# Late attention rows in four banks, the first weight prepared earlier, float32 rows for two second groups

## The chip, the cores and the metric

The kernel runs on one core of a Trainium2 chip. Its engines are TensorE (PE in the profile; its weight loads are PEld), VectorE (DVE), ScalarE (ACT), GpSimd (POOL) and SyncE (SP), which issues most of the transfers. The metric is the device time of one execution in microseconds. The kernel before took 896.62 us as the median of three runs (895.96 to 898.36).

## What is computed

Three stages follow each other. N is 2304 tokens, in 18 tiles of 128.

```
a    = softmax(phi over the 576 positions)           # 4 batches, 8 heads, 32 memory slots
k_m, v_m = a^T k, a^T v
x    = softmax(q k_m^T / 8) v_m                      # 2304 x 512
noisy = x w_gate + log1p(exp(x w_noise)) * noise     # 2304 x 8
top 2 of 8 experts for each token, weights by softmax over the two
y    = sum over the two: weight * relu(x w1[e]) w2[e]    # w1 512 x 1024, w2 1024 x 512
h    = y w_in;  out = (h * cos h) w_out              # w_in 512 x 2048, w_out 2048 x 512
```

Wide products run as three float16 products: each operand is split into a high and a low half, and high*high, high*low and low*high are added.

## The kernel before

**Attention.** `k_gen(b)` builds the memory of a batch; `t_gen(t)` takes a tile of tokens through eight steps: scores on TensorE (`sc`, L734), maximum and subtraction on VectorE (L739, L742), exponential on ScalarE, row sums and reciprocal on VectorE (L747, L748), division on GpSimd (`d`, L750), transposes on TensorE (`pt`), and the product with the values (`x`, L764), whose last 16 columns of each half are the logits of the gate. `x` lies in one tile of two PSUM banks. ScalarE then copies the row (`xs`, L769) and the logits (`lgb`, L775), writes the high half (`hl`, L780), GpSimd subtracts for the low half (L782), and SyncE stores both halves as one row of 2 KB in the DRAM tensor `xd` (L783).

**Routing.** `route(g)` works for two groups of tokens, tiles 0 to 7 (group 0) and 8 to 17 (group 1). On VectorE it is a chain of some thirty small instructions on 64 or 80 elements per partition (L420 to L482), broken by an exponential and a logarithm on ScalarE and by three rank products on TensorE (L461 to L463), which wait for `m16` (L453). Then one-hot matrices (`oha`, L496; `ohp`, L501, two for each tile) are multiplied on TensorE (`tab`, L505) into lists of token numbers: `idxA` (L510) at the end of group 0, `idxB` (L513) at the end of group 1. The first 256 tokens of each expert come from group 0 (part 0), the next 352 from both groups (part 1).

**First expert.** `gather_x(0, 0)` fetches the rows that `idxA` names (GpSimd issues one indirect DMA for 128 rows, L913), and SyncE issues DMA transposes into `xT` (L916). `l1(0, 0, f)` for f = 0 to 7 issues 12 products `h` each (four k, three half-products). Their weight is `wt[0]`: squares of `raw` on ScalarE (`w_square`, into `junk`), a sum on TensorE (`sums`), four tiny instructions for the scale (`norm_scale`), four high quarters on ScalarE (`w_hi`) and four low quarters on VectorE (`w_lo`, x4). `l1_out` applies relu on ScalarE and takes the low half on VectorE (`hT`). `l2_first` multiplies by the second weight `wt[1]`, whose `w_lo` run at 120.31 us. Then come `gather_x(0, 1)` and `l1(0, 1, f)`, the same for part 1, and seven more experts, whose weights are prepared beside the products.

**What sets the order.** Closures are put on a list with a time (`at`), and issued in the order of that time; `lead` raises an instruction's priority. `gated(key)` makes what is issued inside it come after the instruction noted in `last[key]`; `chain(key, ...)` keeps a whole sequence in order on its engine. So each engine has one fixed order of instructions, and an instruction whose operand is late holds everything behind it on its engine. Around the change the order is set by `t_steps`, `AHEAD`, `e0_after`, the `advance(r0, ...)` lines and the offsets behind `tA`, the nominal end of attention.

**Buffers.** `lp` (`l2k`) has seven slots of 2 KB per partition, which `xs`, `hl`, the junk tile and the outputs share; `wp` has four of 16 KB, for phi, q and the weights. PSUM has eight banks: two `ke`, `kt`, `m`, and until attention ends four for `sc`, `pt` and `x`, which then become `ha`, `hb`, `ya`, `yb`.

Of the kernel before, what the change touches and what calls it, by code (L numbers as in the profile page):

```python
# [39 lines left out]
MAXOV = 28  # L40
Y0 = MAXOV * P
# [24 lines left out]
def fused_kernel(ctx, tc, phiT, qT, kv, wgn, noise, w1, w2, wi, wo, out):  # L66
# [3 lines left out]
    xd = nc.dram_tensor("xd", (N, 2 * DM), F16).ap()  # L70
    yd = nc.dram_tensor("yd", (YROWS, DM), F32).ap()
# [341 lines left out]
    def route(g):  # L413
# [68 lines left out]
        V.scalar_tensor_tensor(pf[:, ts, :], af16[:, ts, :], float(-P), vk, op0=OP.mult, op1=OP.add)  # L482
# [9 lines left out]
        for t in range(t0, t1, 3):  # L492
            m = min(3, t1 - t)
            tt = slice(t, t + m)
            oha = small.tile([P, 3, 2, E * NST], F16, tag="oha", name="oha", bufs=2)[:, :m, :, :nc_]
            V.tensor_tensor(oha, acode[:, None, None, c0:].to_broadcast([P, m, 2, nc_]),  # L496
                            af16[:, tt, :, None].to_broadcast([P, m, 2, nc_]), op=OP.is_equal)
            for q in range(m):
                ohp = small.tile([P, 2, P], F16, tag="ohp", name="ohp", bufs=5)
                for k in range(2):  # L500
                    o = V.tensor_scalar(ohp[:, k], iota_r, pf[:, t + q, k:k + 1], tokb[:, t + q:t + q + 1],  # L501
                                        op0=OP.is_equal, op1=OP.mult)
                    last[f"ohp{g}"] = o
                    with gated(f"t{NT - 1 - (g == 0)}P"):
                        last[f"tab{g}_{t + q - t0}"] = T.matmul(  # L505
                            tb[:, :nc_], lhsT=ohp[:, k], rhs=oha[:, q, k], start=(t + q == t0 and k == 0),
                            stop=(t + q == t1 - 1 and k == 1))
            yield
# [120 lines left out]
    def k_gen(b):  # L629
# [69 lines left out]
        A.activation(bv[:, :, 256:272], pw, AF.Copy)  # L699
# [19 lines left out]

    sds = [ap.tile([P, H, M + 1], F32, name=f"sd{k}", tag=f"sd{k}", bufs=1) for k in range(4)]  # L720
# [7 lines left out]
    def t_gen(t):  # L728

        sc = scb[:, t % 2]  # L730
        for p0, n, b in segs(t):
            c0 = (t % 8) * P + p0
            for c in range(4):
                T.matmul(sc[p0:p0 + n, 64 * c:64 * c + 64], lhsT=qt[t // 8][:, c, c0:c0 + n],  # L734
                         rhs=bdkt[b][:, c, :], start=True, stop=True)
        yield
        sv = sc.rearrange("p (h m) -> p h m", m=M)
        mx = ap.tile([P, H], F32, tag="smx", name="smx")
        V.tensor_reduce(mx, sv, axis=AX.X, op=OP.max)  # L739
        dk = sds[t % 4]  # L740
        dv = dk[:, :, 0:M]
        V.tensor_tensor(dv, sv, mx[:, :, None].to_broadcast([P, H, M]), op=OP.subtract)  # L742
        yield
        A.activation(dv, dv, AF.Exp, scale=0.125)
        yield
        su = ap.tile([P, H], F32, tag="ssm", name="ssm")
# [12 lines left out]
        x = aps.tile([P, 2, 512], F32, tag="x", name="x")  # L759
        with gated(f"t{ahead}T" if ahead else f"tab0_{NA - 1}" if t == NT - 1 else None):  # L760
            for p0, n, b in segs(t):
                pn = slice(p0, p0 + n)
                for g in range(2):
                    last[f"t{t}P"] = T.matmul(x[pn, g, 0:272], lhsT=eT[:, g, pn], rhs=bdv[b][:, g, :], start=True,  # L764
                                              stop=True)
        yield
        xs = l2k([P, DM], F32, "xs")
        with gated(f"t{ahead}E"):
            A.activation(xs.rearrange("p (g d) -> p g d", g=2), x[:, :, 0:256], AF.Copy,  # L769
                                          scale=sT[:, 0, t:t + 1] if len(segs(t)) > 1 else sbs[segs(t)[0][2]][:, 0:1])  # L770
# [4 lines left out]
        last[f"t{t}A"] = A.activation(lgb[g][:, t - GROUPS[g][0]], x[:, :, 256:272], AF.Copy)  # L775
        yield
        hl = l2k([P, 2 * DM], F16, "hl")
        hv = hl.rearrange("p (w d) -> p w d", w=2)
        with gated({NT - 2: f"t{NT - 1}A", NT - 1: "ln"}.get(t)):
            A.activation(hv[:, 0], xs, AF.Copy)  # L780
        with gated("gather" if t >= NT - 2 else None):
            G.tensor_tensor(hv[:, 1], xs, hv[:, 0], op=OP.subtract)  # L782
        SP.dma_start(xd[t * P:(t + 1) * P, :], hl)  # L783
        yield

    def load_small():
# [4 lines left out]
    t_steps = (0.0, 1.1, 2.1, 2.8, 4.6, 7.2, 8.0, 8.4)  # L791
    AHEAD = (9, 10, 11, 13, 14, 15, 16)
# [3 lines left out]
        (w_square, 0): ("t7A", "t8A", "t9A", "t10A"),  # L796
        (w_hi, 0): ("t12A", "t13A", "t14A", "t15A"),
        (w_lo, 0): ("ohp0", "idxA", "idxA", "idxA"),
        (w_square, 1): ("t16A", "ln", "ln", "ln"),
        (w_hi, 1): ("ln", "ln", "ln", "ln"),  # L800
        (w_lo, 1): ("idxB", "idxB", "idxB", "idxB"),
    }

    def e0(fn, i, c):

        with gated(e0_after[fn, i][c]):
            fn(i, c)

    def e0_scale(i):
        with gated(("t11P", "t17P")[i]):  # L810
            sum_up(i, 4)
        norm_scale(i, 4)
# [23 lines left out]
    for i in range(NT):  # L836
        g = t_gen(i)
        stages(g, [a_of(i) + x for x in t_steps[:-1 if i >= NT - 2 else None]])
        if i >= NT - 2:
            at(a_end - 0.4499 + 0.0001 * (i - NT + 2), next, g, None, lead=a_end - 0.45 - a_of(i) - t_steps[-1])  # L840
    R1, tA, LA = a_end - 0.5, a_end - 0.45, 60.0
    r0 = route(0)
    for t, n in ((12, 7), (13, 7), (14, 6)):
        at(a_of(t) + 3.0, advance, r0, n, f"t{t}V", f"bdk{B - 1}V")
    at(a_of(17) + 4.75, advance, r0, 99, "t16V", lead=4.5)
    whole(R1, route, 1)
    for c in range(4):
        at(a_of(7 + c) + 8.0, e0, w_square, 0, c)
        at(a_of(12 + c) + 8.0, e0, w_hi, 0, c)
        at(a_of(17) + 7.3 + 0.01 * c if c < 2 else tA + 0.0001 * c, e0, w_lo, 0, c)  # L850
# [4 lines left out]
        at(tA + (0.0017, 0.0018, 0.0025, 0.0035)[c], e0, w_hi, 1, c)  # L855
        at(tA + 0.0096 + 0.00001 * c, e0, w_lo, 1, c)
    at(a_of(11) + 7.0, e0_scale, 0)
    at(tA + 0.0015, e0_scale, 1)


# [45 lines left out]
    def gather_x(e, part, turn=True):  # L906
# [3 lines left out]
        for c in range(c0, c1):  # L910
            g = xg[e, c] = xp.tile([P, 2 * DM], F16, tag="xg", name="xg", bufs=3)
            col = e * (c1 - c0) + c - c0
            last["gather"] = G.indirect_dma_start(out=g, out_offset=None, in_=xd[0:NA * P] if part == 0 else xd,  # L913
                                 in_offset=bass.IndirectOffsetOnAxis(ap=idx[:, col:col + 1], axis=0))
            if turn:
                tr = SP.dma_start_transpose(out=xT[e, part][:, :, (c - c0) * P:(c - c0 + 1) * P], in_=g)  # L916
        if e == 0:
            last["load"] = tr

# [4 lines left out]
    def l1(e, part, f):  # L924
        n = width[part]
        if f == 0:
# [6 lines left out]
        ph = prod[e, part, f] = bank_h()  # L933
        w = wt[2 * e]
        for k in range(4):
            fs = slice(k * F + f * P, k * F + (f + 1) * P)
            with gated("rank" if f else f"t{NT - 1}P") if (e, part, k) == (0, 0, 0) and f in (0, 1) else nullcontext():
                chain("P", T.matmul, ph[:, :n], lhsT=w[:, 0, fs], rhs=x[:, k, :], start=(k == 0), stop=False)
            chain("P", T.matmul, ph[:, :n], lhsT=w[:, 0, fs], rhs=x[:, 4 + k, :], start=False, stop=False)
            chain("P", T.matmul, ph[:, :n], lhsT=w[:, 1, fs], rhs=x[:, k, :], start=False, stop=(k == 3))  # L940
# [60 lines left out]
    def overflow():  # L1001
# [4 lines left out]
        with tc.For_i(0, n, 1, iteration_sync="staggered") as u:  # L1006
# [4 lines left out]
            for t in range(NT):  # L1011
                for k in range(2):
# [10 lines left out]
            G.indirect_dma_start(out=g, out_offset=None, in_=xd,  # L1023
                                 in_offset=bass.IndirectOffsetOnAxis(ap=io[:, :1], axis=0))
            xh = l2k([P, 8, P], F16, "oxh")
            SP.dma_start_transpose(out=xh, in_=g)
# [236 lines left out]
    at(tA + 0.0094, next_pools)  # L1263
    at(tA, gather_x, 0, 0, lead=LA)
    for f in range(8):
        at(tA + 0.002 + 0.001 * f, l1, 0, 0, f, lead=LA)
        at(tA + 0.002 + 0.001 * f, l1_out, 0, 0, f, lead=LA)
    for c in range(CA):
        at(tA + 0.0095 + 0.003 * c, l2_first, c, False, f"tab1_{NG - 1}", lead=LA)
# [23 lines left out]
    at(x - 0.05, gather_x, 0, 1)  # L1293
    at(x - 0.04, gather_x, 1, 0)
    for e in range(E):
# [15 lines left out]
        if e == 0:  # L1311
            at(x + 0.1, gather_x, 1, 1)
# [134 lines left out]
    OV, LP, PRE = 13.0, 16.0, 30.0  # L1447
    for c in range(2 * NCH):
# [61 lines left out]
```

## Time and profile before

| | us |
|---|---|
| median of three runs | 896.62 (895.96 to 898.36) |
| the profiled execution's own time | 897.48 |
| its span, first to last instruction | 895.5 |
| PE busy in the span | 861.0 (96%) |
| mean granted TensorE clock | 0.978 of full speed |

The span is what the trace shows from the first to the last instruction; the time of the execution is 1.98 us longer. The page shows the span in 40 slices of 22.4 us. Attention ends at 94.3 us, the products of the first expert begin at 103.8 us, and those of its second part at 129.7 us. From 160 us on TensorE has no idle slice before the last one.

### The profile page before, as it was taken

To read this page: it belongs to the slowest core of one execution; us is meant where nothing else is said; L and a number is where in the kernel's file an instruction comes from. 1 tells how busy PE (TensorE), PEld (TensorE's weight loads), DVE (VectorE), ACT (ScalarE), POOL (GpSimd) and SP (SyncE) were. 2 spreads that over 40 slices of the span, in tenths; PEclk is the share of its full clock that TensorE was granted. 3 is DMA by queue.
4 is the path that set the end of the run, shared out by engine and by line. 5 is a ranking of instruction groups with operands and counts; after the bars stand their busy time and mean duration, and the time that the engine had idled before them with its cause. 6 is when DMAs were issued, how large, how long until landed. Compare 5 with 4: busy or idle time off the path is not lost.

```text
span 895.5 us, 16091 instructions
## 1 busy us (share of the span) xinstructions
PE 861.0 (96%) x6328; PEld 523.5 (58%) x6328; DVE 584.1 (65%) x1248; ACT 465.0 (52%) x830; POOL 214.7 (24%) x242
## 2 busy tenths in 40 slices
PE   5997599999999999999999999999999999999997
PEld 3875355757566574757566576654444444444564
DVE  3559853775668576866752389999877654465564
ACT  3588526566677677667762345453434322322233
POOL 1355321110111102010101154443532222222221
PEclk9898599999999999999999999999999999999999
DMA  9982459879989879796963623331522001100001
GB/s 350 395 329 83 129 159 224 293 221 314 221 298 272 275 237 309 251 322 252 258 253 133 196 71 83 71 94 48 119 58 61 25 0 24 48 1 1 1 24 47
DMA packets 109629, 146.66 MB, mean 164 GB/s; under 512 B 65776, under 2 KB 68720, under 8 KB 107504
## 3 DMA queue, kind: packets, MB, share of 16 engines
q1 hardware_dynamic: 89840, 103.95, 37.9%
q0 software_dynamic: 6080, 19.93, 7.7%
q10 hardware_dynamic: 13632, 21.74, 6.7%
q8 instruction: 50, 0.82, 0.4%
q14 instruction: 27, 0.22, 0.1%
HBM read 95.26 MB, written 35.13 MB: 146 GB/s over the span
## 4 chain that ended last, share of the span: by engine, by line
PE 85%; DVE 7%; ACT 4%; issue 2%; DMA 1%; ACTq 1%; SPq 0%; POOL 0%; DVEq 0%
PE y L289 22%; PE h L289 20%; PE g L289 19%; PE o L289 18%; PE kp L664 1%; DVE tt L289 1%; DMA kvt<-in_kv 1%; PE sc L734 1%; DVE ty L289 1%; PE x L764 1%; ACT junk L289 1%; ACT tt L289 1%; DVE ohp L501 1%; PE sums L289 1%; ACTq L289 1%
## 5 line engine op out<-in xcount | busy, mean ns | idle before, releaser
L289 PE MATMUL h<-x,w 128*128 128x352 f16 (+1 forms) x1536 | 205.2, 295 | 0.8 <-DVE hT L289 0.6
L289 PE MATMUL y<-w,hT 128*128 128x512 f16 (+2 forms) x1920 | 203.2, 294 | 1.1 <-issue 0.5
L289 PE MATMUL g<-x2T,win 128*128 128x256 f16 (+1 forms) x1152 | 202.2, 326 | 0.0
L289 PE MATMUL o<-wout,gT 128*128 128x512 f16 x864 | 201.5, 379 | 0.0
L289 PEld LDWEIGHTS <-w 128*128 128x128 f16 x1536 | 151.2, 99 | 49.6 <-issue 1.0
L289 PEld LDWEIGHTS <-win 128*128 128x128 f16 x1152 | 112.6, 98 | 83.7
L289 PEld LDWEIGHTS <-hT 128*128 128x128 f16 (+2 forms) x1920 | 106.3, 100 | 92.3 <-issue 3.6
L289 POOL TENSOR_TENSOR gT<-ty,gT 128x256 f16<-128x256 f32 (+1 forms) x96 | 90.8, 946 | 245.1 <-ACT gT L289 244.9
L289 ACT ACTIVATE tt<-tt,hp 128x256 f32<-128x256 f32 (+1 forms) x96 | 59.0, 615 | 158.4 <-DVE tt L289 151.9
L289 PEld LDWEIGHTS <-gT 128*128 128x128 f16 x864 | 84.5, 98 | 91.9
L289 DVE SCALAR_TENSOR_TENSOR hT<-h,hT 128x352 f16<-128x352 f32 (+1 forms) x128 | 59.4, 470 | 70.6 <-ACT hT L289 65.0
L289 DVE SCALAR_TENSOR_TENSOR ty<-g,wis,bct 128x256 f32<-128x256 f32 (+1 forms) x96 | 58.8, 613 | 63.8 <-PE g L289 62.4
L289 DVE SCALAR_TENSOR_TENSOR w<-raw,wsc,w 128x1024 f16<-128x1024 f32 x64 | 80.9, 1278 | 18.1 <-ACT w L289 15.9
L289 DVE SCALAR_TENSOR_TENSOR ty<-g,fac,tt 128x256 f32<-128x256 f32 (+1 forms) x96 | 59.0, 615 | 45.3 <-ACT tt L289 44.5
L289 ACT ACTIVATE hT<-h 128x352 f16<-128x352 f32 (+1 forms) x128 | 53.5, 421 | 64.4 <-PE h L289 51.1
L289 ACT ACTIVATE gT<-ty 128x256 f16<-128x256 f32 (+1 forms) x96 | 50.2, 523 | 61.3 <-DVE ty L289 57.3
L913 POOL DMA_INDIRECT xg<-xd,idxB x24 | 26.4, 1100 | 209.2 <-DMA x<-xg 196.3
L289 ACT ACTIVATE w<-raw,wsc 128x1024 f16<-128x1024 f32 x64 | 72.0, 1142 | 3.8 <-ACT o L289 3.8
L289 DVE SCALAR_TENSOR_TENSOR tt<-tt,ty 128x256 f32<-128x256 f32 (+1 forms) x96 | 69.6, 725 | 3.0
L289 ACT ACTIVATE junk<-raw 128x1024 bf16<-128x1024 f32 x64 | 67.3, 1052 | 3.8 <-ACT o L289 3.3
L289 ACT ACTIVATE o<-y,ysc 128x512 f32<-128x512 f32 (+1 forms) x40 | 26.6, 665 | 63.1 <-PE y L289 60.4
L289 POOL DMA_INDIRECT y<-yd,sidx x36 | 35.9, 998 | 82.5 <-DMA yd<-o 75.6
(230 smaller groups left out, 714.9 us busy)
## 6 DMA issues: line engine op xcount, KB each, us to landing
raw<-in_w SPq DMA_DIRECT2D x32, 1024.0 KB
kvt<-in_kv SPq DMA_DIRECT2D x9, 1024.0 KB
yd<-o ACTq DMA_DIRECT2D x32, 256.0 KB
cvt<-in_wi SPq DMA_DIRECT2D x8, 1024.0 KB
wst<-cvt SPq DMA_DIRECT2D x16, 512.0 KB
cvt<-in_wo SPq DMA_DIRECT2D x8, 1024.0 KB
yd<-zero ACTq DMA_DIRECT2D x14, 512.0 KB
xd<-hl SPq DMA_DIRECT2D x18, 256.0 KB
```

Source lines behind the costliest of these rows:

```text
L289: last[key] = fn(*a, **kw)
L501: o = V.tensor_scalar(ohp[:, k], iota_r, pf[:, t + q, k:k + 1], tokb[:, t + q:t + q + 1], op0=OP.is_equal, op1=OP.mult)
L664: T.matmul(kp[32 * j:32 * j + 32, g, :], lhsT=es[i][:, 32 * h:32 * h + 32], rhs=kvv[:, :, h * D:(h + 1) * D], start=(i == 0), stop=(i == 4))
L734: T.matmul(sc[p0:p0 + n, 64 * c:64 * c + 64], lhsT=qt[t // 8][:, c, c0:c0 + n], rhs=bdkt[b][:, c, :], start=True, stop=True)
L764: last[f"t{t}P"] = T.matmul(x[pn, g, 0:272], lhsT=eT[:, g, pn], rhs=bdv[b][:, g, :], start=True, stop=True)
L913: last["gather"] = G.indirect_dma_start(out=g, out_offset=None, in_=xd[0:NA * P] if part == 0 else xd, in_offset=bass.IndirectOffsetOnAxis ...
```

## The change

- **Four banks.** Tiles 10, 12, 14 and 16 (`APART`) put `x` into the two `ke` banks, one for each half, instead of the two-bank tile, so that two successive tiles have four banks. The copies `xs` and `lgb` become two instructions each for these tiles. Tile 17 copies its logits ahead of `xs`. Both tiles 16 and 17 now have their `x` products behind group 0's `tab` products (before: tile 17 alone).
- **First weight.** The squares, high quarters and low quarters of `wt[0]` have other gates: three tiles earlier for squares and high quarters (the scale behind `t15S`, the subtraction of tile 15), and the four low quarters spread over group 1's routing (after `ohp0`, `u`, `m161`, `pf1`).
- **Routing of group 0** starts behind the subtraction of tile 15 with two steps; ten more follow behind that of tile 17, the rest behind tile 17's reciprocal. Before, 20 of its steps lay between tiles 12 and 14.
- **Float32 rows.** `xs` is stored in a second DRAM tensor `xf` for all 18 tiles. Tiles 10 to 17 keep `xs` in one `wp` buffer (`kept`); their high and low halves are made and stored during expert 0's second part (`split_late`, `store_late`). Part 1 of experts 0 and 1 is gathered from `xf`, split on ScalarE and VectorE (`split`), then transposed.
- **High products in front.** For f = 0 to 5 the 8 products with the high weight go first, into six banks, and the 4 with the low weight follow. f = 6 and 7 stay whole. The `tab` products of group 1 stand at fixed places among them, and the token number is multiplied into `oha` on ScalarE instead of into `ohp` on VectorE.
- The overflow loop splits its row itself; the transposes of expert 1's part 0 are placed by hand.

```diff
             for q in range(m):
+                if g:
+                    A.activation(oha[:, q], oha[:, q], AF.Copy, scale=tokb[:, t + q:t + q + 1])
...
-                    o = V.tensor_scalar(ohp[:, k], iota_r, pf[:, t + q, k:k + 1], tokb[:, t + q:t + q + 1],
-                                        op0=OP.is_equal, op1=OP.mult)
+                    o = V.tensor_scalar(ohp[:, k], iota_r, pf[:, t + q, k:k + 1],
+                                        None if g else tokb[:, t + q:t + q + 1], op0=OP.is_equal,
+                                        **({} if g else dict(op1=OP.mult)))
...
-        x = aps.tile([P, 2, 512], F32, tag="x", name="x")
-        with gated(f"t{ahead}T" if ahead else f"tab0_{NA - 1}" if t == NT - 1 else None):
+        if t in APART:
+            x = [trp("x")[:, None] for g in range(2)]
+        else:
+            xb = aps.tile([P, 2, 512], F32, tag="x", name="x")
+            x = [xb]
+        with gated(f"t{ahead}T" if ahead else None), gated(f"tab0_{NA - 1}" if t == NT - 2 else None):
...
+        xs = kept[0][:, t - NK] if t >= NK else l2k([P, DM], F32, "xs")
...
+        SP.dma_start(xf[t * P:(t + 1) * P, :], xs)
+        if t < NK:
             hl = l2k([P, 2 * DM], F16, "hl")
             A.activation(hv[:, 0], xs, AF.Copy)
             G.tensor_tensor(hv[:, 1], xs, hv[:, 0], op=OP.subtract)
             SP.dma_start(xd[t * P:(t + 1) * P, :], hl)
...
-        (w_square, 0): ("t7A", "t8A", "t9A", "t10A"),
-        (w_hi, 0): ("t12A", "t13A", "t14A", "t15A"),
-        (w_lo, 0): ("ohp0", "idxA", "idxA", "idxA"),
+        (w_square, 0): ("bdv2A", "t4A", "t5A", "t6A"),
+        (w_hi, 0): ("t9A", "t10A", "t11A", "t12A"),
+        (w_lo, 0): ("ohp0", "u", "m161", "pf1"),
         (w_square, 1): ("t16A", "ln", "ln", "ln"),
-        (w_hi, 1): ("ln", "ln", "ln", "ln"),
-        (w_lo, 1): ("idxB", "idxB", "idxB", "idxB"),
+        (w_hi, 1): ("A", "A", "A", "A"),
+        (w_lo, 1): ("ohp1", "idxB", "idxB", "idxB"),
...
-    for t, n in ((12, 7), (13, 7), (14, 6)):
-        at(a_of(t) + 3.0, advance, r0, n, f"t{t}V", f"bdk{B - 1}V")
-    at(a_of(17) + 4.75, advance, r0, 99, "t16V", lead=4.5)
-    whole(R1, route, 1)
+    at(a_of(15) + 1.2, advance, r0, 2, "t15S", lead=5.0)
+    at(a_of(17) + 1.2, advance, r0, 10, "t17S", lead=7.0)
+    at(a_of(17) + 2.9, advance, r0, 8, "t17V", lead=5.0)
+    at(a_of(17) + 4.75, advance, r0, 99, "t17V", lead=4.5)
+    r1 = route(1)
+    at(R1, advance, r1, 1, "idxA")
+    at(R1 + 0.0005, advance, r1, 15, "lo01")
+    at(tA + 0.00205, advance, r1, 1, "P")
+    at(tA + 0.00206, advance, r1, 4, "lo02")
+    for i in range(4):
+        at(tA + (0.00468, 0.00498, 0.0081, 0.0082)[i], advance, r1, 1, "lo03")
+    at(tA + 0.0083, advance, r1, 99)
...
+            raw = part and e < 2
+            G.indirect_dma_start(out=g.bitcast(F32) if raw else g, out_offset=None,
+                                 in_=xf if raw else xd if part else xd[0:NA * P],
...
+    def split(e, c):
+        x = xg[e, c].bitcast(F32)
+        xg[e, c] = l2k([P, 2 * DM], F16, "xh")
+        hv = halves(xg[e, c])
+        chain("A", A.activation, hv[:, 0], x, AF.Copy)
+        chain("V", V.tensor_tensor, hv[:, 1], x, hv[:, 0], op=OP.subtract)
+        turn_x(e, 1, c)
...
+    at(tA + 0.0091, gather_x, 0, 1, False, lead=49.0)
+    for c in range(CA, NST):
+        at(tA + 0.0092 + 0.00005 * (c - CA), split, 0, c, lead=49.0)
+    for f in range(6):
+        at(tA + 0.002 + 0.0001 * f, l1, 0, 0, f, False, lead=LA)
+        at(tA + 0.0045 + 0.0001 * f, l1, 0, 0, f, True, lead=LA)
...
+    for i in range(NT - NK):
+        t = X[0] + 0.2 + 3.6 * i
+        at(t, split_late, NK + i)
+        at(t + 3.2, store_late, NK + i)
```

## Rows read from the trace of the kernel before

**Rows 1.** The page's 40 slices: TensorE's busy tenths, its granted clock, GB/s moved.
```profile
PE   5997599999999999999999999999999999999997
...
PEclk9898599999999999999999999999999999999999
GB/s 350 395 329 83 129 159 224 293 221 314 221 298 272 275 237 309 251 322 252 258 253 133 196 71 83 71 94 48 119 58 61 25 0 24 48 1 1 1 24 47
```
**Rows 2.** Windows by stage: length, busy us (instructions) by engine, clock, DMA share, GB/s.
```profile
60.00:75.00 15.00, 13.21 (x113) 10.98 (x112) 10.72 (x31) 14.77 (x42) 8.57 (x12) 1.00 0.37 138
75.00:95.00 20.00, 13.72 (x60) 8.44 (x58) 19.11 (x64) 13.60 (x30) 9.36 (x10) 0.67 0.21 80
95.00:103.40 8.40, 0.02 (x1) 0.02 (x1) 7.59 (x16) 4.90 (x12) 5.05 (x4) 0.50 0.57 144
129.80:160.00 30.20, 29.73 (x295) 18.46 (x293) 9.60 (x16) 18.85 (x32) 6.03 (x7) 1.00 0.94 257
```
**Rows 3.** The chain of waits in order of time: start, us, what.
```profile
93.34 3.58 DVE w L289 x3
...
102.17 1.16 ACT junk L289 x2
...
103.97 2.58 PE h L289 x12
...
118.20 1.32 PE h L289 x12
119.52 10.36 PE y L289 x48
129.88 10.74 PE h L289 x72
```
**Rows 4.** Timeline of VectorE: start, us, line, operation, tiles, count, idle before.
```profile
78.54 0.41 DVE L742 TENSOR_TENSOR sd<-sc,smx 128x256 f32<-128x256 f32 x1
...
82.03 1.17 DVE L453 TENSOR_TENSOR m<-oh,oh 128x64 f16<-128x64 f32 x1
...
91.01 0.97 DVE L501 TENSOR_SCALAR ohp<-iota_r,pf,tokb 128x128 f16<-128x128 f16 x4
91.90 1.27 DVE L289 SCALAR_TENSOR_TENSOR w<-raw,wsc,w 128x1024 f16<-128x1024 f32 x1
93.09 0.16 DVE L510 TENSOR_SCALAR idxA<-tab 128x16 int32<-128x16 f32 x1
...
105.55 0.24 DVE L453 TENSOR_TENSOR m<-oh,oh 128x80 f16<-128x80 f32 x1
...
118.24 0.18 DVE L513 TENSOR_TENSOR idxB<-tab,tabB 128x24 int32<-128x24 f32 x1 [0.93 <-PE tab L505]
```
**Rows 5.** Timeline of GpSimd: a low half of `hl`, and three gathers.
```profile
81.97 1.15 POOL L782 TENSOR_TENSOR hl<-xs,hl 128x512 f16<-128x512 f32 x1
...
93.55 2.03 POOL L913 DMA_INDIRECT xg<-xd,idxA  x1 [3.64 <-DVE tabB L511]
95.88 2.11 POOL L913 DMA_INDIRECT xg<-xd,idxA  x1 [0.30 <-issue]
...
118.69 0.98 POOL L913 DMA_INDIRECT xg<-xd,idxB  x1 [7.89 <-DVE idxB L513]
```
**Rows 6.** Timeline of TensorE: the last scores and the last values of attention.
```profile
75.77 1.10 PE L734 MATMUL sc<-bdk,qt 128*128 128x64 f32 x8 [0.37 <-DVE sd L742]
...
92.13 2.15 PE L764 MATMUL x<-bdv,e2T 128*128 128x272 f32 x4
```
**Rows 7.** Waits of TensorE up to 160 us: us in total, times, longest.
```profile
PE sc L734 <- DVE sd L742: 2.2, 3, 1.2
```
**Rows 8.** SyncE's timeline, the transposes of part 1: start, us.
```profile
122.08 4.53 SPq L916 DMA_TRANSPOSE x<-xg  x3
```
**Rows 9.** The tiles `hl` (60 to 104 us) and `xd`: durations ns min/median/max; time to landing.
```profile
L780 ACT ACTIVATE hl<-xs x11: 613/629/652, 63.2 to 100.5; 128x512 f16<-128x512 f32 x11
...
DMA to landing us min/median/max: 4.4/6.9/7.8
```

More of the change, by code (lines that the diff above doesn't have):

```diff
@@ L481, in route @@
         V.tensor_scalar(af16[:, ts, :], af[:, ts, :], MAGIC, MAGIC, op0=OP.add, op1=OP.subtract)
-        V.scalar_tensor_tensor(pf[:, ts, :], af16[:, ts, :], float(-P), vk, op0=OP.mult, op1=OP.add)
+        last[f"pf{g}"] = V.scalar_tensor_tensor(pf[:, ts, :], af16[:, ts, :], float(-P), vk, op0=OP.mult, op1=OP.add)
         G.tensor_copy(af[:, ts, :], af16[:, ts, :])
@@ L745, in t_gen @@
         yield
-        su = ap.tile([P, H], F32, tag="ssm", name="ssm")
+        su = ap.tile([P, H], F32, tag="ssm", name="ssm", bufs=4)
         V.tensor_reduce(su, dk, axis=AX.X, op=OP.add)
@@ L763, in t_gen @@
                 for g in range(2):
-                    last[f"t{t}P"] = T.matmul(x[pn, g, 0:272], lhsT=eT[:, g, pn], rhs=bdv[b][:, g, :], start=True,
+                    last[f"t{t}P"] = T.matmul(xh(g)[pn, 0:272], lhsT=eT[:, g, pn], rhs=bdv[b][:, g, :], start=True,
                                               stop=True)
         yield
[L767 to L770, printed above, removed]
         g = ROUTE_OF[t]
@@ L854, in fused_kernel @@
             at(a_of(17) + 8.0, e0, w_square, 1, c)
[L855 to L858, printed above, removed]
+        at(tA + 0.00231 + 0.00001 * c, e0, w_hi, 1, c)
+        at(tA + (0.0084, 0.0089, 0.00922, 0.00932)[c], e0, w_lo, 1, c)
+    at(a_of(15) + 1.3, e0_scale, 0, lead=8.0)
+    at(tA + 0.00204, e0_scale, 1)
     pools = {}
@@ L922, in turn_x, with first_bank, l1 @@
         chain("load", SP.dma_start_transpose, out=xT[e, part][:, :, (c - c0) * P:(c - c0 + 1) * P], in_=xg[e, c])
-    def l1(e, part, f):
+    def first_bank(f):
+        return pools["ps"].tile([P, 512], F32, tag=("yb", "ya")[f - 4], name="h", bufs=1) if f in (4, 5) else bank_h()
+    def l1(e, part, f, low=None):
         n = width[part]
-        if f == 0:
+        if f == 0 and not low:
             if part == 0:
@@ L932, in l1 @@
         x = xT[e, part][:, :, :n]
-        ph = prod[e, part, f] = bank_h()
+        ph = prod[e, part, f] = prod[e, part, f] if low else first_bank(f) if e + part == 0 else bank_h()
         w = wt[2 * e]
@@ L936, in l1 @@
             fs = slice(k * F + f * P, k * F + (f + 1) * P)
[L937 to L940, printed above, removed]
+            if not low:
+                with gated({0: f"t{NT - 1}P", 1: "rank"}.get(f) if (e, part, k) == (0, 0, 0) else None):
+                    chain("P", T.matmul, ph[:, :n], lhsT=w[:, 0, fs], rhs=x[:, k, :], start=(k == 0), stop=False)
+                chain("P", T.matmul, ph[:, :n], lhsT=w[:, 0, fs], rhs=x[:, 4 + k, :], start=False, stop=False)
+            if low is not False:
+                chain("P", T.matmul, ph[:, :n], lhsT=w[:, 1, fs], rhs=x[:, k, :], start=False, stop=(k == 3))
     def l1_out(e, part, f):
@@ L1292, in fused_kernel @@
     x = X[0]
-    at(x - 0.05, gather_x, 0, 1)
-    at(x - 0.04, gather_x, 1, 0)
+    at(x - 0.04, gather_x, 1, 0, False)
+    for c in range(CA):
+        at(x + 8.5, turn_x, 1, 0, c)
     for e in range(E):
@@ L1311, in fused_kernel @@
         if e == 0:
-            at(x + 0.1, gather_x, 1, 1)
+            at(x + 0.1, gather_x, 1, 1, False)
+            for c in range(CA, NST):
+                at(x + 6.0 + 0.8 * (c - CA), split, 1, c, lead=0.0)
         elif e < E - 1:
```

97 lines of the change are left out of this document (68 added, 29 removed).

## The prediction, made before the changed kernel was run

> **What bounds the kernel now.** I read the slices first, then windows around the place where TensorE has holes, the chain of waits through it, and the timelines of the engines that the chain names. The slices show TensorE full from slice 8 on, and holes in slices 4 to 6, 67 to 134 us; its clock falls to half in slices 4 and 5 [rows 1]. The windows split this: ScalarE is full from 60 to 75 us (14.77 of 15), VectorE from 75 to 95 (19.11 of 20), and TensorE then does nothing for 8.4 us [rows 2]. The chain says the same: VectorE's low quarters, ScalarE's squares, then the first `h` at 103.97 us, and from 118.20 us products without a gap, `y` for 10.36 us and part 1's `h` at 129.88 [rows 3]. All that follows is products end to end, so the change is worth what it moves that last start: **I count everything at the start of `h` of part 1.** It has two feeders: TensorE's own work from the first `h`, and the rows that `idxB` names, 118.42 us in the old trace [rows 4], 11.4 us before.
>
> **Routing of group 0.** What makes VectorE full is partly waiting. At 82.03 us `m16` takes 1.17 us; the same instruction of group 1, with more elements, takes 0.24 at 105.55 [rows 4]. A low half of `hl` runs on GpSimd from 81.97 for 1.15 us [rows 5] and both end together. Between 67 and 93 us there are eight such pairs, one for each tile from 8 to 15, on average some 0.85 us of delay: 7 us. The change moves the subtractions of tiles 10 to 15 off this stage (six, 5.1 us), and the two of tiles 8 and 9 meet no routing any more, which starts later.
>
> *By the Trainium skill, "SBUF — State Buffer", section "SBUF: two separate sides", GpSimd and a VectorE instruction with two SBUF inputs or in a two-port mode lock one port pair, and the later blocks until the other is done; the trace agrees, 1.17 against 0.24 us. The rule also speaks against the change: `split` and the second weight's `w_lo` are such instructions, and stand beside the gathers of part 1. That is taken up as a rival below, from rows.*
>
> Against the gain stands that most of routing now begins only when tile 17's subtraction is done. That ended at 78.95 us [rows 4], though its scores began at 75.77 and took 1.10 [rows 6]; free of routing the 0.75 us of maximum and subtraction follow at once. TensorE had waited 2.2 us for such subtractions [rows 7]; these, too, go with the routing steps, so I take them whole: scores end at 76.87 - 2.2 = 74.7, subtraction at 75.5. (Lower bound: none of the 2.2, 77.6.) From there, in VectorE's order: 20 small instructions at 0.23 us (0.24 in [rows 4]) and a slow reciprocal, 4.9; the rank products' round trip 0.5; ten more at 0.19, 1.9; three `oha` at 0.3 and 16 `ohp` at 0.24 (four in 0.97 [rows 4]), 4.8; the sums of tiles 16 and 17, 0.9; two divisions on GpSimd that still block, 0.4. Sum 13.4, last `ohp` at 88.9. It was 91.98. The low quarter and `idxA` behind it keep their 1.27 us [rows 4]: `idxA` ends at 90.2 instead of 93.25, **3.0 us sooner** (bounds 0.9 and 4.5, the latter if routing also loses its waits for ScalarE).
>
> ScalarE loses `hl` of tiles 10 to 15 here, six of 0.63 us [rows 9], and gains five short instructions for the halved copies. The squares and high quarters of `wt[0]` are moved, not added: ScalarE is short between 60 and 75 us and not before, so they are worth up to 2.5 us there; since TensorE was busy 13.21 of those 15 us [rows 2], the room is 1.8, already contained in the 2.2. I add nothing, nor for the four banks (the same wait seen from the other side).
>
> **First expert.** The two first gathers took 2.03 and 2.11 us on GpSimd, one of part 1 only 0.98 [rows 5]. The low quarters stood beside the slow ones (93.34, 3.58 us [rows 3]). Three of them leave this place, so the second gather is issued about 2.2 us earlier. The first `h` came 10.7 us after `idxA`, now 8.5: 98.7 us instead of 103.97. The first 24 products run at half clock, 2.58 us for 12 against 1.32 [rows 3]; I expect that again, since TensorE idles about as long. Splitting the products into 8 and 4 adds none, and six banks mean no wait for `l1_out`.
>
> This 5 us is not what reaches the end. Tiles 16 and 17 now have their values behind `tab`: two times 2.15 us at half clock [rows 6], to 93.6, and the logits of tile 17 feed group 1's routing at 94. It then takes 0.6 us to `u`, a low quarter of 1.27, and 20 instructions at 0.275, 6.1 us: `m16` at 102. Before, it was 105.8, so the rank products come 4 us sooner, behind the first 8 high products and the second weight's sum, whose squares need 3.5 us after the logarithm and are done by 100. From there to `idxB` it was 11.9 us. One low quarter now falls into the wait for the rank, one behind `pf` (+1.27), against VectorE's wait of 0.93 before `idxB` [rows 4], which goes; `oha`'s product on ScalarE adds 0.2 where VectorE goes on with `ohp`. I take 12.6: `idxB` at 115.0, **3.4 us sooner** (bounds 1 and 5). TensorE waits for `tab` at most 1 us in f = 6 and 7, then has one `h` of 1.31 and the `y` of 10.36: ready at 126.6, 3.3 sooner.
>
> The rows of part 1 take a new step: ScalarE's high half 0.63 [rows 9] and VectorE's low half, for which no row stands (512 float32 elements less 512 float16: above 0.42 for 256 elements, below 1.27 for 1024 [rows 4]; I take 0.6), so 1.3 with the handovers. The three overlap behind the first, since the transposes need 1.5 each (4.53 for three [rows 8]). These rows used to land up to 0.6 before they were used. So they are ready 3.4 - 1.3 + 0.6 = **2.7 us sooner**, and this is the later feeder.
>
> **Outside this stage.** 18 stores of 256 KB to `xf` are added, each about 0.65 us of all the DMA engines at the 400 GB/s that they reach where they are full [rows 1]; on SyncE's queue they stand ahead of the stores to `xd` and of the first transposes, and only the latter are waited for, with every `xs` done by then. From 60 to 95 us these are busy 0.37 and 0.21 of the time [rows 2]. Before 60 us they are nearly full: tiles 0 to 6 add 4.6 us of transfers there, which delays the loads issued behind them. A row also holds its slot until its store has landed, 6.9 us [rows 9], where GpSimd let it go before: three tiles at 3.5 us each pass in 10.5 us, which about covers it. Cost 0, at worst 3. `split_late` gives ScalarE 8 * 0.63 = 5.0 us and VectorE 4.8 between 130 and 160 us, where they are busy 18.85 and 9.60 of 30.2; without that cover an `h` bank would come late by 0.6 us a piece. Its stores (2.1 MB) and the waits of `store_late` on SyncE stand before weights that are wanted 10 us or more after they land; DMA is at 0.94 there [rows 2]. Cost 0, at worst 2.
>
> **The sum.** 897.48 - 2.7 = 894.8 for the profiled execution (span 895.5 plus 1.98), which lies 0.86 above the median; from the median, **896.62 - 2.7 = 893.9 us**. About 0.3%, 2.7 us, is also what a measurement of this kernel can tell from no change.
>
> **Rivals.**
> *The clock stays up.* The values of the late tiles no longer wait for their banks, and tiles 16 and 17 put 4.3 us of products into the gap, so the idle stretch is short and the first 24 products cost 1.32 per 12: 2.5 us more, and tile 17's logits come 2 us sooner, which moves `idxB` by about as much. For it: TensorE has work for 13.7 of the 20 us from 75 to 95. Against: it still waits some 5 us for the gathers, and its clock is 0.50 throughout the idle window before [rows 2]. Time 896.62 - 2.7 - 2.8 = 891.
>
> *The gathers of part 1 are blocked.* The second weight's low quarters now follow `ohp1` and `idxB` directly, beside the gathers and in front of `split`. For it: the gathers beside low quarters took 2.03 against 0.98 us [rows 5]. Against: only one gather is likely to meet one that has begun. Price 1.1 for a gather and 1.2 for a `split` behind a quarter: 2.3, leaving 0.4: 896.2. (The Trainium skill's port rule, above, would have every one of these meetings block.)
>
> *The late start of routing decides: slower.* Routing waits for `t17S`, while VectorE idles before. If scores come no earlier (subtraction done at 78.95 as before), `idxA` ends at 78.95 + 13.4 + 1.27 = 93.6, `idxB` at 118.8, and the new split with the blocked gather and the queue costs 1.3 + 2.3: `h` of part 1 starts at 118.8 + 11.4 + 3.6 = 133.8 against 129.88. It decides once the subtraction ends after 77.7 us. For it: VectorE had 4.3 us free from 60 to 75 that nothing now fills [rows 2]. Against: tile 17's own scores were held back by routing. Time 900.5.
>
> *The change doesn't do what it says:* long VectorE instructions stay long without `hl`, because of the divisions `d`: then 5.1 us of waiting remain less what the later start avoids, time 897 to 899.
>
> **How the numbers follow.** Forecast 0.46, with a range of its own of 892.0 to 895.6; its lower half is faster by over 0.3%. Clock stays up 0.20, blocked gathers 0.15, late routing 0.14, not as said 0.05. Faster: 0.23 + 0.20 + a little from the forecast's spread, 0.45. Slower: 0.14 and half of the last, with the transfers outside the stage, 0.18. The same: 0.37. The range for 8 in 10, from the clock case and its spread to between blocked gathers and late routing: 889.8 to 898.6.
>
> **What would show it.** Right: `m16` near 0.25 us, last `ohp` near 89, both first gathers near 1 us, first `h` near 98.7, `idxB` near 115.0, `h` of part 1 at 127.2 and waiting for transposes, not for `y`. Wrong: tile 17's subtraction after 77.7; ScalarE waiting for raw weights or a slot before 60 us; a wait of TensorE after 130 us that the trace of before doesn't have; or a first `h` whose lead is lost in the `tab` products.

## The result, and the profile after

The changed kernel took **903.72 us** (median of five; 902.2 to 904.92) against 896.62 of before, timed beside it: ratio 1.0073, 95% interval 1.0054 to 1.0093, **slower by 0.7%**. Forecast were 893.9 us and a range up to 898.6: the sign is wrong and the time lies outside. The profiled execution took 903.2, with a span of 901.1.

One caution for the two traces. Executions reach the attention at different times after the span's start, so I subtract one common instruction, the third exponential of the memories' softmax on ScalarE. Before, after, and the run with both mends (below), one row each:

```profile
31.17 0.78 ACT L642 ACTIVATE ew<-ph,mx 128x576 f32<-128x576 f32 x1
```
```profile
30.11 0.78 ACT L650 ACTIVATE ew<-ph,mx 128x576 f32<-128x576 f32 x1
```
```profile
31.12 0.78 ACT L650 ACTIVATE ew<-ph,mx 128x576 f32<-128x576 f32 x1
```

Timeline of VectorE after, against [rows 4]: the subtraction of tile 17, `m16`, `idxA`, `m16` of group 1, `idxB`.

```profile
77.42 0.43 DVE L751 TENSOR_TENSOR sd<-sc,smx 128x256 f32<-128x256 f32 x1 [5.18 <-POOL d L759]
...
84.08 0.22 DVE L455 TENSOR_TENSOR m<-oh,oh 128x64 f16<-128x64 f32 x1
...
93.49 0.17 DVE L518 TENSOR_SCALAR idxA<-tab 128x16 int32<-128x16 f32 x1
...
102.01 0.24 DVE L455 TENSOR_TENSOR m<-oh,oh 128x80 f16<-128x80 f32 x1
...
116.60 0.18 DVE L521 TENSOR_TENSOR idxB<-tab,tabB 128x24 int32<-128x24 f32 x1
```

`m16` is short now, as forecast, but the subtraction stands where it stood (47.3 us behind the common row, before 47.4) and `idxA` is 1.5 us later (63.4 against 61.9). The windows, against [rows 2], say where it went wrong: from 60 to 75 us VectorE and TensorE are busy for less time (7.21 and 11.54 us, before 10.72 and 13.21), and the transfers for more (0.59, before 0.37).

```profile
60.00:75.00 15.00, 11.54 (x83) 8.76 (x81) 7.21 (x22) 12.35 (x32) 7.06 (x10) 0.84 0.59 229
75.00:95.00 20.00, 14.39 (x78) 10.39 (x76) 14.84 (x63) 15.76 (x42) 6.93 (x11) 0.86 0.38 141
```

SyncE issues the first two stores to `xf` here:

```profile
41.85 2.14 SPq L803 DMA_DIRECT2D xf<-xs  x2
```

The timeline of ScalarE shows what they cause: tile 3's row is written at 44.48, but its high half comes at 56.26 and tile 4's row at 56.98. The same instructions before stand below them.

```profile
44.48 0.69 ACT L798 ACTIVATE xs<-x,sb 128x512 f32<-128x512 f32 x1
...
56.26 0.62 ACT L807 ACTIVATE hl<-xs 128x512 f16<-128x512 f32 x1
56.98 0.69 ACT L798 ACTIVATE xs<-x,sT 128x512 f32<-128x512 f32 x1
```
```profile
45.63 0.69 ACT L769 ACTIVATE xs<-x,sb 128x512 f32<-128x512 f32 x1
...
48.35 0.64 ACT L780 ACTIVATE hl<-xs 128x512 f16<-128x512 f32 x1
...
49.76 0.69 ACT L769 ACTIVATE xs<-x,sT 128x512 f32<-128x512 f32 x1
```

`xs` and `hl` of tiles 0 to 2 and `xs` of tile 3 fill the seven slots. By the program's instruction list, `hl` of tile 3 takes the slot of tile 0's `xs` and waits for the first of those stores to land. The trace's landing events, assigned by that list, put the three raw loads ahead of the store at 49.23, 51.80 and 54.39 us and the store itself at 55.09, 13.2 us after its issue. In the trace ScalarE does not stand idle for it: the order of its instructions is fixed when the program is built, and there a dozen later ones have moved ahead of this `hl`, which runs 1.2 us after the landing.

The first expert wins that back: its `h` of part 1 starts 98.1 us behind the common row (before 98.6), the second expert's first `h` 127.4 (before 128.7). Then the second loss. The chain of waits after, against [rows 3], in order of time: start, us, what.

```profile
103.23 1.87 PE h L291 x8
...
117.89 10.36 PE y L291 x48
128.24 10.83 PE h L291 x72
...
159.20 7.04 DMA raw<-in_w
...
166.32 0.39 ACTq L291
...
166.75 0.39 ACT hT L291
...
167.17 0.43 DVE hT L291
...
167.65 2.50 PE h L291 x11
```

TensorE stands 4.72 us in the middle of the second expert's products (its timeline below); the eleven behind take 2.50 us where [rows 3] has twelve in 1.32. What it waits for is `hT` on ScalarE, and that stands in the queue behind a store of zeros to `yd` (ACTq at 166.32), which is issued only when a 1 MB load of raw weights has landed. In the program's instruction list the transfers of SyncE and ScalarE share eight counters in turn: each is issued only when the one eight before it has landed. The eight added `store_late` shifted who stands eight behind whom: before, the zeros stood behind a transpose.

```profile
167.65 4.64 PE L291 MATMUL h<-x,w 128*128 128x256 f16 x21 [4.72 <-DVE hT L291]
```

### The profile page after: what moved, and what is told of

Its sections match the earlier page's. It is cut to its first block, busy times and chain, and to the rows that moved or that the text cites. A ratio compares the mean times of both kernels' runs of the same rounds, so it can differ in the third digit from the quotient of the medians.

```text
span 901.1 us, 16149 instructions
## 1 busy us (share of the span) xinstructions
PE 859.8 (95%) x6328; PEld 522.9 (58%) x6328; DVE 583.8 (65%) x1263; ACT 472.3 (52%) x854; POOL 204.7 (23%) x234
## 4 chain that ended last, share of the span: by engine, by line
PE 84%; DVE 5%; ACT 4%; DMA 4%; issue 2%; ACTq 1%; POOL 0%; SPq 0%; DVEq 0%
PE y L291 21%; PE h L291 19%; PE g L291 19%; PE o L291 18%; PE sc L743 2%; DVE tt L291 1%; PE x L778 1%; PE kp L672 1%; DMA kvt<-in_kv 1%; ACT w L291 1%; DVE ty L291 1%; DMA raw<-in_w 1%; ACT tt L291 1%; ACTq L291 1%; DMA x<-xh 1%
## 5 line engine op out<-in xcount | busy, mean ns | idle before, releaser
L291 PEld LDWEIGHTS <-win 128*128 128x128 f16 x1152 | 112.7, 98 | 83.7
L291 DVE SCALAR_TENSOR_TENSOR hT<-h,hT 128x352 f16<-128x352 f32 (+1 forms) x128 | 59.3, 470 | 65.4 <-ACT hT L291 59.5
L291 DVE SCALAR_TENSOR_TENSOR ty<-g,wis,bct 128x256 f32<-128x256 f32 (+1 forms) x96 | 58.8, 612 | 63.3 <-PE g L291 59.2
L291 ACT ACTIVATE hT<-h 128x352 f16<-128x352 f32 (+1 forms) x128 | 53.3, 421 | 61.2 <-PE h L291 47.3
L950 POOL DMA_INDIRECT xg<-xd,idxB x18 | 19.8, 1099 | 192.8 <-DMA x<-xg 179.8
```

The source lines that it names most:

```text
L291: last[key] = fn(*a, **kw)
L950: G.indirect_dma_start(out=g.bitcast(F32) if raw else g, out_offset=None, in_=xf if raw else xd if part else xd[0:NA * P], in_offset=bass. ...
```

## Experiments

Ratios are against the kernel before, timed beside each, with 95% intervals. Where a distance "by the ratios" is given, it is the difference of two such ratios.

**Zeros later.**
```diff
-        at(X[1] + 10.0 * u, clear, u)
+        at(X[1] + 6.0 + 10.0 * u, clear, u)
```


> The changed kernel with one edit: the stores of zeros to yd, which ScalarE issues, come 6 us later in the order, behind the four hT and three w_hi of the same engine that they stood in front of. Theory A (the store of zeros waits until the 1 MB load of raw weights issued at 159.20 has landed, and ScalarE's queue stands behind it): the 4.72 us hole of TensorE before 167.65 us and the half-clock products behind it go, h of expert 1 part 0 starts near 157.5 and its y is no longer late: 4.7 to 7.3 us less than the changed kernel, 896.5 to 899. Rival B (ScalarE is late because the raw weights themselves are late, or because GpSimd's hT or a slot is): the hole stays within 1 us, 902.5 to 904.

897.49 us, ratio 1.002 (1.0004 to 1.0036): 6.2 us less by the medians, 4.8 by the ratios. Theory A holds. Of the hole 2.04 us remain, because two stores of `o` stand eight behind an `o` store and the third transpose (ACTq 3.37 us). TensorE's and ScalarE's timelines:

```profile
166.11 6.08 PE L291 MATMUL h<-x,w 128*128 128x256 f16 x39 [2.04 <-DVE hT L291]
```
```profile
161.80 3.37 ACTq L291 DMA_DIRECT2D yd<-o  x2
```

**No row held by the store.**
```diff
-        SP.dma_start(xf[t * P:(t + 1) * P, :], xs)
+        if t >= NK:
+            SP.dma_start(xf[t * P:(t + 1) * P, :], xs)
...
             SP.dma_start(xd[t * P:(t + 1) * P, :], hl)
+            SP.dma_start(xf[t * P:(t + 1) * P, :], hl.bitcast(F32))
```


> The changed kernel, but for tiles 0 to 9 the store to xf takes the bytes of hl (halves) in place of the float32 row xs, and is issued behind hl: same number of stores and bytes, but no xs is held by one. It leaves out the float32 rows of tiles 0 to 9, so that gathers from xf read other values there. Theory S (attention is late because xs and hl wait for slots whose store of xs has not landed): hl of tile 3 runs within 2 us of its xs (now 11.8 us behind), tile 7's row comes near 62 instead of 69.4, subtraction of tile 17 near 75.5 instead of 77.4, idxA 1.5 to 2 us sooner; total 901 to 903, since the wait near 163 us stays. Rival T (the traffic of 18 more stores among the weight loads delays the attention, whoever holds the slot): tile 7's row stays at 68 to 70 and idxA near 93.5, total 903 to 904.

901.16 us, ratio 1.0046 (1.0031 to 1.0062). With the zeros later too:

> Both edits of the two runs before (zeros 6 us later; store to xf of tiles 0 to 9 from hl, so their float32 rows are left out). If A and S both hold: 894 to 897, about the forecast of 893.9 plus what the split costs. If A alone: as the first run, 896.5 to 899. If neither: 902.5 to 904.

896.0 us, ratio 0.9992 (0.998 to 1.0003). Each gains some 2.5 us by the ratios over its partner, and `xs` of tile 4 comes at 48.30, but `idxA` gains only 1 to 2 us: `hl` now has two stores to wait for, and from the row at 57.65 on the wait is back. Inconclusive between slots and traffic: the edit moved the hold.

**The second weight behind the rows' stores, zeros later.**
```diff
+    def late_load(i, h):
+        with gated(f"xf{4 + h}"):
+            w_load(i, h)
...
-            at(37.1 + 0.1 * (2 * i + h), w_load, i, h, lead=37.0)
+            if i:
+                at(62.0 + 0.1 * h, late_load, i, h)
+            else:
+                at(37.1 + 0.1 * h, w_load, i, h, lead=37.0)
...
-    put_weights(2, (tA - 12.0, tA + 0.0001), X[0] + 1.0, 0.0)
+    put_weights(2, (62.3, tA + 0.0001), X[0] + 1.0, 0.0)
```


> Everything is computed. Zeros 6 us later as in the first run, and the loads of the second weight are issued only behind the stores to xf of tiles 4 and 5, so that the stores of the first tiles do not queue behind those megabytes. If the slots are held because the stores wait in the DMA queues behind raw weights (theory Q): hl of tile 3 runs near 46 to 50 us, tile 7's row at 62 to 64, and idxA 1 to 2 us sooner than 93.5; total 894.5 to 898. If the stores are slow for another reason, rows stay late and the total is that of the first run or 1 to 2 us more, since the second weight lands later: 897 to 901.

**891.29 us**, ratio 0.9936 (0.9922 to 0.995): faster than both kernels, 3 us below the range expected. The total came out better than the rows: `hl` of tile 3 at 53.16 and tile 7's row at 64.42 (before 60.17, after 69.37) are later than expected, so the gate shortens the hold and does not end it. The first store now has two raw loads ahead of it and lands at 52.40. The timelines of ScalarE, VectorE and TensorE:

```profile
53.16 0.62 ACT L807 ACTIVATE hl<-xs 128x512 f16<-128x512 f32 x1
...
64.42 0.68 ACT L798 ACTIVATE xs<-x,sb 128x512 f32<-128x512 f32 x1
```
```profile
74.78 0.42 DVE L751 TENSOR_TENSOR sd<-sc,smx 128x256 f32<-128x256 f32 x1
...
90.64 0.17 DVE L518 TENSOR_SCALAR idxA<-tab 128x16 int32<-128x16 f32 x1
...
111.42 0.18 DVE L521 TENSOR_TENSOR idxB<-tab,tabB 128x24 int32<-128x24 f32 x1
```
```profile
87.50 1.18 PE L778 MATMUL x<-bdv,e2T 128*128 128x272 f32 x4
...
99.23 1.87 PE L291 MATMUL h<-x,w 128*128 128x256 f16 x8 [9.46 <-DMA x<-xg]
...
123.28 1.95 PE L291 MATMUL h<-x,w 128*128 128x352 f16 x12
```

**The gate alone** (the zeros line put back):

> The changed kernel with the second weight's loads issued behind the xf stores of tiles 4 and 5, and nothing else; the zero stores stay where the change has them. Everything is computed. Theory (two separate losses): attention is early again as in the run with both edits (idxA near 90.6 us, h of part 1 near 123.3), but the store of zeros still waits for the raw weights and TensorE stands 4 to 5 us behind it: 896.5 to 898, some 6 us above the 891.3 of both edits. Rival (the wait for the raw weights was there only because attention was late): 891 to 893.

897.61 us, ratio 1.0008 (0.9997 to 1.0018). The hole is there again, 4.79 us, though the rows are early: the two losses are separate. By the ratios the zeros are worth 6.5 us here, and the gate 5.8 us (without later zeros) to 7.5 (with them). The kernel before was not run with the gate.

```profile
163.09 20.26 PE L291 MATMUL h<-x,w 128*128 128x256 f16 x132 [4.79 <-DVE hT L291]
```

**The kernel before with eight row stores, and with eight copies instead.**
```diff
+        if t < 8:
+            SP.dma_start(xf[t * P:(t + 1) * P, :], xs)
         hl = l2k([P, 2 * DM], F16, "hl")
```


> The kernel before, with the eight xf stores of tiles 0 to 7 added (256 KB each, issued by SyncE when the row xs is written) and nothing else; nobody reads them. Everything is computed. Theory (rows hold their slots until stores that stand behind megabytes of weights have landed): tile 7's row comes at 65 to 70 us in place of 60.17, tile 17's subtraction ends 1 to 3 us after 78.95, and the total is 898 to 900.5. Rival (2 MB of more traffic is hidden, and the slots were never short): rows within 1 us of before, total 896 to 897.5.

903.18 us, ratio 1.0064 (1.0049 to 1.0078): 6 us for eight stores that nobody reads, where the theory gave 1.4 to 3.9. The other one:
```diff
-        SP.dma_start(xd[t * P:(t + 1) * P, :], hl)
+        last["xds"] = SP.dma_start(xd[t * P:(t + 1) * P, :], hl)
+        if t < 8:
+            chain("xds", SP.dma_start, xf[t * P:(t + 1) * P, :], w1[7][0:P, 0:DM])
```


> The kernel before with eight transfers of 256 KB to xf added, one behind the xd store of each tile from 0 to 7, that copy a piece of a weight from DRAM to DRAM: the traffic of the run with the eight row stores, but no row held. Nobody reads them; everything is computed. Slot theory (the rows were late because xs cannot be overwritten until its store has landed): tile 7's row and idxA within 1.5 us of before, total 896.5 to 898.5. Traffic theory (2 MB more among the weights delays attention whoever holds what, as the halves' own stores land later): idxA 4 to 6 us later as with the row stores, total 901 to 903.5.

895.36 us, ratio 0.9993 (0.9979 to 1.0007): the same bytes, and as many more transfers to count, for nothing, 1.1 us below the range expected. So neither the bytes nor the count of transfers costs here; what is left is the held slot. (The copies also differ in that each stands behind the `xd` store and reads DRAM.) `idxA` is 59.2 us behind the common row, 2.8 sooner than before, where I expected 1.5 at most; its order of instructions differs from 61 us on. How much of those 2.8 us is the edit's and how much is chance isn't shown. ScalarE's rows around tile 3, with the stores, where the first of them lands at 55.14, and then with the copies:

```profile
44.25 0.69 ACT L770 ACTIVATE xs<-x,sb 128x512 f32<-128x512 f32 x1
56.08 0.62 ACT L783 ACTIVATE hl<-xs 128x512 f16<-128x512 f32 x1
```
```profile
46.48 0.69 ACT L770 ACTIVATE xs<-x,sb 128x512 f32<-128x512 f32 x1
49.20 0.64 ACT L781 ACTIVATE hl<-xs 128x512 f16<-128x512 f32 x1
```

**Four banks undone, on the version with both mends.**
```diff
-    APART = (10, 12, 14, 16)
+    APART = ()
```


> The version with both edits (gate and later zeros, 891.3 us), with the values of tiles 10, 12, 14 and 16 back in the banks that all tiles use; everything else, and all results, as there. The prediction gave the four banks nothing: then 890.5 to 892.5, tile 17's subtraction within 0.5 us of 74.8. Rival (the late tiles catch up only by the four banks): tile 16's or 17's values wait for a bank, idxA 1 to 3 us later than 90.6, total 892.5 to 894.5.

894.46 us, ratio 0.9974 (0.9956 to 0.9993), 3.4 us above its base by the ratios (by their intervals 1 to 6). The subtraction did not move later (43.0 us behind the common row, base 43.7), and `idxA` hardly (0.4). The late tiles' values and logits did: tile 17's logits are read 60.4 us behind the common row, below. Five profiles here have the same order of instructions up to `idxB` (both mends, the gate alone, and the last three runs on those two below); they have these logits at 57.1 to 58.1 and `idxB` at 79.3 to 81.3. Without the banks `idxB` is at 82.2. So the banks are worth some 3 us by the times, at another place than the rival said; of this 1 to 3 us are seen at `idxB`.

```profile
90.38 0.20 ACT L789 ACTIVATE rt<-x 128x32 f32<-128x32 f32 x1 [0.24 <-PE x L778]
```

**Products whole, on the version with both mends.**
```diff
-        (w_lo, 0): ("ohp0", "u", "m161", "pf1"),
+        (w_lo, 0): ("ohp0", "idxA", "idxA", "idxA"),
...
-        at(tA + 0.002 + 0.0001 * f, l1, 0, 0, f, False, lead=LA)
-        at(tA + 0.0045 + 0.0001 * f, l1, 0, 0, f, True, lead=LA)
+        at(tA + 0.0045 + 0.0001 * f, l1, 0, 0, f, lead=LA)
```


> The version with both edits (891.3 us), with the first expert's products of part 0 whole again (high and low together for each f) and the first weight's three low quarters right behind idxA, as in the kernel before; everything is computed. The prediction's price: the gathers stand beside low quarters and take near 2 us each in place of 1.16 and 0.96, the first h comes 2.2 us later than 99.2, idxB 1.2 to 2.5 later than 111.4: total 893 to 894.5. Rival (the products in front are worth nothing, because y bounds part 1): 891 to 892.

897.35 us, ratio 1.001 (0.9998 to 1.0023): 6.6 us more than its base by the ratios, where 1.7 to 3.2 were expected. GpSimd's and VectorE's timelines:

```profile
89.29 2.26 POOL L957 DMA_INDIRECT xg<-xd,idxA  x1 [6.12 <-DVE tabB L519]
91.85 2.03 POOL L957 DMA_INDIRECT xg<-xd,idxA  x1 [0.30 <-issue]
```
```profile
88.83 0.17 DVE L518 TENSOR_SCALAR idxA<-tab 128x16 int32<-128x16 f32 x1
...
102.77 0.32 DVE L468 TENSOR_TENSOR_SCAN rt<-same,rank 128x80 f32<-128x80 f16 x1 [3.03 <-PE rank L465]
...
116.08 0.18 DVE L521 TENSOR_TENSOR idxB<-tab,tabB 128x24 int32<-128x24 f32 x1 [0.66 <-PE tab L291]
```

The slow gathers cost the 2.2 us that I gave them (first `h` 10.9 us behind `idxA`, base 8.6): beside low quarters they took 2.26 and 2.03 us, in the base 1.16 and 0.96. By the Trainium skill, "SBUF — State Buffer", section "SBUF: two separate sides", the two engines lock one port pair against each other; these rows agree. What I left out is TensorE's queue: the rank and `tab` products of group 1 stand behind whole `h` products, which wait for low quarters, gathers and `hT`; VectorE waits 3.03 us for the rank, and `idxB` comes 27.3 us behind `idxA` (base 20.8).

**The late stores on GpSimd's queue**, on the changed kernel, on the gate alone, and on both mends:
```diff
-        chain("load", SP.dma_start, xd[t * P:(t + 1) * P, :], late.pop(t))
+        G.dma_start(xd[t * P:(t + 1) * P, :], late.pop(t))
```


> The changed kernel with one edit: the eight late stores to xd (store_late) are issued by GpSimd's queue in place of SyncE's, same bytes and place in the program; zeros and everything else stay. Theory (a transfer of SyncE's or ScalarE's waits for the one eight before it, and the added stores moved the zero store onto the raw weights): the zero store now stands eight behind the third transpose, the hole of 4.72 us before 167.65 shrinks to about 2 us (the wait that the run with later zeros showed, for that transpose), total 897 to 899.5. Rival (ScalarE waits for the traffic of the late stores and the weights, whichever counts them): the hole stays at 4 to 5 us, total 902 to 904.

899.78 us, ratio 1.0038 (1.0025 to 1.0051); hole 1.99 us, as the theory said, the total 0.3 us above its range.

> The version with the gate alone (897.6 us, zeros where the change has them), with the eight late stores issued by GpSimd's queue. Everything is computed. By the same theory the hole falls from 4.79 us to 2 or less: total 890.5 to 893. By the rival it stays: 896.5 to 898.

893.79 us, ratio 0.9971 (0.9957 to 0.9985); hole 1.92 us, the total again just above. TensorE's timeline in these two:

```profile
166.91 19.60 PE L291 MATMUL h<-x,w 128*128 128x256 f16 x132 [1.99 <-DVE hT L291]
```
```profile
161.36 18.41 PE L291 MATMUL h<-x,w 128*128 128x256 f16 x132 [1.92 <-DVE hT L291]
```

The bytes are the same and only the queue that issues and counts the stores changed. SyncE also has fewer transfers to issue, but the hole that is left is the one that the counters give, so I take the waits to be those of the counters.

> The version with gate and later zeros (891.3 us), with the eight late stores issued by GpSimd's queue. Left there is a hole of 2.06 us, which two stores of o on ScalarE cause that stand eight behind an o store and the third transpose. If the transposes come sooner when SyncE no longer issues the late stores: hole under 1 us, total 889.5 to 890.8. If not: 890.8 to 892.5 (a late store on GpSimd also blocks it for about a us each, which nothing waits for here).

891.84 us, ratio 0.9949 (0.9933 to 0.9966): the hole is gone, the total is not better, a miss by 1 us. In the profile `sums` now waits twice, 0.56 and 0.34 us, for squares on ScalarE. `idxB` is 1.0 us later behind the common row, but that is no effect of the edit: the order of instructions is the same up to there, and the granted clock from 100 to 105 us was 0.50 in this profile and 0.75 in the base's.

**The two small stores of `o` on SyncE, on the version with both mends.**
```diff
-                chain("A", A.dma_start, yd[r0 + r:r0 + r + m, :].rearrange("r (q n) -> q r n", n=n), o[:, col:col + n])
+                chain("A", A.dma_start if e else SP.dma_start, yd[r0 + r:r0 + r + m, :].rearrange("r (q n) -> q r n", n=n), o[:, col:col + n])
```


> The version with gate and later zeros (891.3 us), with the two small o stores at the end of the first expert issued by SyncE in place of ScalarE. Everything is computed. If the remaining hole of 2.06 us is ScalarE standing in these two stores: it goes, and the total is 889 to 890. If something else is late next (GpSimd's or the transposes' own): 890.5 to 892.

**887.93 us** (886.45 to 888.83), ratio 0.9904 (0.9887 to 0.9921), the best of all and 1 us below the range expected: the products of the second expert run through. The profiled execution is the fastest of the five, and its `idxB` is 1.0 us sooner than the base's already, ahead of the edit; so not all of the 2.9 us by the ratios need be the stores'.

```profile
150.42 23.17 PE L291 MATMUL h<-x,w 128*128 128x256 f16 x180
```

## Why the prediction was wrong, step by step

Starts in us behind the common row. The prediction's are its times less 31.17; for `idxA` and `idxB`, which it gave by their ends, also less their own 0.16 and 0.18 us.

| | before | predicted | after | both mends |
|---|---|---|---|---|
| `idxA` | 61.9 | 58.9 | 63.4 | 59.5 |
| first `h` | 72.7 | 67.5 | 73.1 | 68.1 |
| `idxB` | 87.1 | 83.7 | 86.5 | 80.3 |
| `h` of part 1 | 98.6 | 96.0 | 98.1 | 92.2 |

**The step that failed is "Outside this stage", in both of its sums.**

*"A row also holds its slot until its store has landed, 6.9 us ... Cost 0, at worst 3."* The 6.9 us of [rows 9] are not a store's: that view counts all transfers of the tensor `xd`, and its landing times are those of five gathers that read it, at 93.5 us and later. For the stores the landing events of the same trace, assigned by the program's instruction list, say 13.2 us for the one issued at 41.70 and 14.5 for the next, and 2.0 for most of those from 65 to 90 us. So the number for this place was in the trace of before, and I had said myself that the transfers are nearly full there. In the changed kernel tile 0's row is written at 33.06, its store is issued at 41.85, behind the raw loads on SyncE, and lands at 55.09: the slot is held for 22 us, six tiles at 3.5 us, where I had let three pass and the seven slots hold the two buffers of three and a half. In three runs with row stores `hl` of tile 3 follows that landing by about 1 us (55.09 and 56.26; 55.14 and 56.08; 52.40 and 53.16). Eight such stores on the kernel before cost 6 us, and the same bytes without the hold nothing. In the changed kernel the hold ate what the routing had won.

*"Its stores ... and the waits of `store_late` on SyncE stand before weights that are wanted 10 us or more after they land ... Cost 0, at worst 2."* I looked at who wants the weights, and not at who stands behind them in the count of eight: ScalarE's store of zeros, and behind that `hT`, without which TensorE has no bank. Cost 4.8 to 6.5 us.

**Routing of group 0** was right where it could be seen: `m16` 0.22 us. The subtraction, forecast to end 3.4 us sooner (75.5 against 78.95: 2.2 with TensorE's waits gone, the rest with the routing steps in front of it), came no sooner for the slots; with both mends it came 3.7 us sooner, and `idxA` within 0.7 us of the forecast. How much of that is the routing's is open: the kernel before with eight copies has the old routing and its `idxA` at 59.2, too.

**First expert.** First `h` 8.5 us behind `idxA` was right with both mends (8.6), not in the changed kernel (9.7), where the second gather met the low quarter at 95.17 and took 1.85 us. `idxB` was sized too late by 3.4 us: I let group 1's routing wait for the last two tiles' values behind `tab`, at half clock until 93.6; with both mends the last ran at 87.50 in 1.18 us for four, before `tab` ended. The high products in front, which I counted only as shorter gathers, also free TensorE's queue for the rank, 6.6 us in all together with the spread low quarters; the four banks, which I gave nothing, are worth some 3.

**The rivals.** "The late start of routing decides" got its condition: the subtraction ended at 77.85, past 77.7. Yet it did not make the kernel slower: the run with later zeros has the same late subtraction (47.3 us behind the common row) and loses 0.2%. Its 900.5 is 3.2 us from the measured time, and for another reason. The gathers of part 1 took 0.96 us each, not blocked. The clock was half again at the first `h`, eight products in 1.87 us, as forecast.

So two costs, entered at nothing, took 12 us. With both mended the kernel is 5 to 6 us faster than before, and 8.7 without the last two stores on ScalarE, where 2.7 were forecast. Since the kernel before was not run with these mends, how much of that is the change's own stays open.

Two smaller readings in the prediction were loose: the clock is at half in slice 5 alone, and TensorE is full from slice 6 on [rows 1].

## What to carry to other kernels

A store that reads a buffer makes its landing time part of the buffer's turn: take that time, from the writing of the buffer to the landing, from stores in the stretch where the new one will stand, behind what is queued there, and count the turns against the slots. Where transfers of several queues share counters in turn, adding some changes which transfer every later one waits for: look for a slow transfer eight before a quick one on a busy engine's queue, and move the quick one away. When a kernel gets slower by a constant step, list TensorE's holes before re-arguing the stage that was changed.

## What the runs showed that I had not expected

- Eight unread stores of 256 KB cost 6 us, the same bytes as copies within DRAM nothing.
- A store of 256 KB took 13.2 us from issue to landing behind three loads of 1 MB (after, issued at 41.85; before, at the same place, 13.2 too). From 65 to 90 us, before, stores of that size mostly took 2.0.
- The common row lay between 29.94 and 32.33 us in the profiles of these kernels, whose work up to there is the same: two traces compared by their absolute times can be wrong by 2 us. Even behind the common row, `idxB` lay between 79.3 and 81.3 us in five profiles with the same order of instructions up to it.
